# The gated experts' second matmul with the activations stationary, summed out of PSUM by VectorE

## The chip, the cores and the metric

One core of a Trainium2 chip runs the whole program. Times are device microseconds of that core. PE is TensorE, DVE is VectorE, ACT is ScalarE, POOL is GpSimd, and SP is the engine whose queue issues the DMAs.

## The reference

There are 1152 tokens of 512 features. They come from an attention with a window of 64 keys (2 sequences of 576, 8 heads of 64). Two feed-forward layers follow:

```
x = attention(q, k, v)                       # 1152 x 512
p = domain_probs / sum(domain_probs)         # 1152 x 4
for e in range(4):                           # gated experts, F = 1024
    out += p[:, e:e+1] * (relu(x @ w1[e]) @ w2[e])
h = out @ w_in                               # 512 -> 2048
return (h * cos(h)) @ w_out                  # 2048 -> 512
```

All is float32, except that `w_in` and `w_out` arrive as float64.

## The kernel before

**Precision.** Each operand of a large matmul is split into two parts, a rounded high part (`hi`) and the rest (`lo`), and a product is three matmuls: high by high, high by low, low by high. ACT makes the high part of each weight (L164, `whi`), and POOL, for all units but one, the low part (L170, `wlo`).

**Passes.** The work is cut into passes (e, g). Index e counts slices of 512 hidden features: 0 to 7 for the gated experts (two for each), 8 to 11 for the last layer. Index g is a group of tokens: group 0 has 256, group 1 has 384, group 2 has 512. Passes 0 and 1 go over the groups one by one, while the attention still makes the later groups' tokens. From pass 2 on each e goes over all three groups, in turn backward and forward, so that two passes over group 0, or two over group 2, follow each other at every turn. Passes 7 and 8 both go forward.

**Steps.** A pass has four steps (f), each of 128 hidden features. `emit_a` is the first matmul of a step: 12 matmuls with the weight stationary and the group's tokens moving (L457 to L459), into one of four PSUM banks of the pool `psa`. The gated experts then take the relu on ACT (`hh`, L466) and its low part on DVE (`hl`, L467). The last layer takes h cos(h) in several pieces (`cos_stages`), and holds its `psa` bank until the product `gg` is made (L491). `emit_b` is the second matmul of a step (L525). It adds into PSUM banks of the pool `psb`, which has four; after the last step `finish` evicts them.

**Orientation of the second matmul.** For e below 8 the weight is stationary and the token group moves: four blocks of 128 output features, each over n tokens, so four banks for any group, and a result with features on the partitions. DVE multiplies each block with a broadcast row of the gate values (L555, at pass 0 L552), and POOL adds it to the sum (L556). The broadcast rows, `pb`, are made from a transposed copy of the gates in DRAM, and loaded by `load_pb` on SP's queue, one for each pass. After pass 7 `split_x` splits the sum, block by block, into the next layer's `xhi` and `xlo` (L534, L535). For e from 8 the activations are stationary and the weight moves: one block of 128 tokens by 512 features for each 128 tokens, so 2, 3 and 4 banks.

**Order.** Every engine works in the order in which the program is written. The order between passes is a fixed sequence of ticks, one for each `emit_a` or `emit_b`:

```
            ("A", i, 2), ("A", i, 3), ("B", i, 0), ("B", i, 1),
            ("A", i + 1, 0), ("B", i, 2), ("A", i + 1, 1), ("B", i, 3),
```

Between the last second matmul of a pass and the first of the next stand two first matmuls. `later(d, fn)` puts a piece of work d ticks behind the present one. `between(part)` is called inside a tick, after a part of its matmuls, and lets in pieces that are due and, in the first 30 ticks, pieces of the attention. From tick 32 on one of the 16 float64 weight units is converted every 9 ticks, by seven DVE instructions (L130 to L153).

Of the kernel before, what the change touches and what calls it, by code (L numbers as in the profile page):

```python
# [8 lines left out]
F32 = mybir.dt.float32  # L9
# [4 lines left out]
ALU = mybir.AluOpType  # L14
# [10 lines left out]
def tile_window_attention_moe_cosglu(  # L25
# [12 lines left out]
    nc = tc.nc  # L38
    P = 128
# [5 lines left out]
    NT = NTOK // P  # L45
    NE, DM, FF = w1.shape
    NP = H // 2
    KD = DM // P
    FE = 512
    NFC = FE // P  # L50
    SPL = FF // FE
    NM = NE * SPL
    NX = NM + w_in.shape[1] // FE
    SCALE = 1.0 / float(D) ** 0.5
    GS = [256, 384, 512]
    G0 = [0, 256, 640]
# [5 lines left out]
    rawp = ctx.enter_context(tc.tile_pool(name="rawp", bufs=4))  # L62
    xp = ctx.enter_context(tc.tile_pool(name="xp", bufs=1))
    hp = ctx.enter_context(tc.tile_pool(name="hp", bufs=5))
    pbp = ctx.enter_context(tc.tile_pool(name="pbp", bufs=2))
    tp = ctx.enter_context(tc.tile_pool(name="tp", bufs=4))
    dramp = ctx.enter_context(tc.tile_pool(name="dramp", bufs=1, space=bass.MemoryType.DRAM))
    psb = ctx.enter_context(tc.tile_pool(name="psb", bufs=4, space=bass.MemoryType.PSUM))
    psa = ctx.enter_context(tc.tile_pool(name="psa", bufs=4, space=bass.MemoryType.PSUM))
# [3 lines left out]
    def bank(name):  # L73
        return psa.tile([P, 512], F32, tag="psa", name=name)
# [168 lines left out]
        nc.sync.dma_start(out=t[:n], in_=v[b, s + W - n:s + W, :])  # L243
        v_t[j] = t

    ident = acon.tile([P, P], F32, name="ident")
    mask = acon.tile([P, 1, 2 * W], F32, name="mask")
    mask0 = acon.tile([P, 1, W], F32, name="mask0")

# [21 lines left out]
    xhi, xlo = {}, {}  # L271
# [98 lines left out]
            nc.vector.tensor_tensor(out=lo, in0=src, in1=hi.bitcast(F32), op=ALU.subtract)  # L370


    pT = dramp.tile([NT * NE, P], F32, name="pT")
    pb_t = {}

    dpn = acon.tile([P, NT, NE], F32, name="dpn")

    def load_gate():
# [2 lines left out]
    def gate():  # L381
        t = dpn
        s = acon.tile([P, NT], F32, name="dps")
        nc.vector.tensor_reduce(out=s, in_=t, op=ALU.add, axis=AX.X)
        nc.vector.tensor_scalar_add(s, s, 1e-09)
        r = acon.tile([P, NT, 1], F32, name="dpr")
        nc.vector.reciprocal(out=r[:, :, 0], in_=s)
        pn = acon.tile([P, NT, NE], F32, name="dpp")
        nc.vector.tensor_tensor(out=pn, in0=t, in1=r.to_broadcast([P, NT, NE]), op=ALU.mult)
        return pn  # L390

    def store_gate(pn):
        ps = bank("psg")
        nc.tensor.transpose(
            out=ps[:NT * NE, :P], in_=pn.rearrange("p c e -> p (c e)"), identity=ident
        )
        pt = acon.tile([P, P], F32, name="dpt")
        nc.vector.tensor_copy(out=pt[:NT * NE], in_=ps[:NT * NE, :P])
        nc.sync.dma_start(out=pT, in_=pt[:NT * NE])

    def load_pb(e, g):
        t = pbp.tile([P, GS[g]], F32, tag="pb", name="pb")
        c0, n = G0[g] // P, GS[g] // P
        src = pT.rearrange("(c e) t -> e c t", e=NE)[e // SPL, c0:c0 + n, :]
        nc.sync.dma_start(
            out=t.rearrange("p (c t) -> p c t", c=n), in_=src.partition_broadcast(P)
        )
        pb_t[e, g] = t


    bias_m = const.tile([P, 1], F32, name="bias_m")
# [26 lines left out]
    def later(d, fn, *args):  # L438
        waiting.append((tick[0] + 1 + d, fn, args))
# [65 lines left out]
    def emit_b(s):  # L505
        e, g, f = steps[s]
        n = GS[g]
        u, fo = divmod(f, 2)
        whi, wlo = w_hi[e, 1, u], w_lo[e, 1, u]
        hh, hl = h_t.pop(s)  # L510
        first, last = f == 0, f == NFC - 1
        no = KD if e < NM else n // P
        if first:
            b_ps[g] = [psb.tile([P, 512], F32, tag="psb", name="pb_acc") for _ in range(no)]
        for i in range(no):
            if e < NM:
                ps = b_ps[g][i][:, :n]
                cs = slice(P * i, P * (i + 1))
                ops = ((whi[:, fo, cs], hh), (whi[:, fo, cs], hl), (wlo[:, fo, cs], hh))
            else:  # L520
                ps = b_ps[g][i]
                cs = slice(P * i, P * (i + 1))
                ops = ((hh[:, cs], whi[:, fo, :]), (hh[:, cs], wlo[:, fo, :]), (hl[:, cs], whi[:, fo, :]))
            for m, (a, b) in enumerate(ops):
                nc.tensor.matmul(  # L525
                    out=ps, lhsT=a, rhs=b, start=first and m == 0, stop=last and m == 2
                )
            between((i + 1) / no)
        if last:
            finish(e, g)  # L530

    def split_x(g, i):
        a = acc_x[g][:, i, :]
        nc.scalar.copy(out=xhi[g][:, i, :], in_=a)  # L534
        nc.vector.tensor_tensor(  # L535
            out=xlo[g][:, i, :], in0=a, in1=xhi[g][:, i, :].bitcast(F32), op=ALU.subtract
        )

    def finish(e, g):
        n = GS[g]  # L540
        pss = b_ps.pop(g)
        if e < NM:
            pb = pb_t.pop((e, g))
            if e == 0:
                acc[g] = xp.tile([P, KD, n], F32, tag=f"acc{g}", name="acc")
            if e == NM - 1:
                x_tiles(g)
                acc_x[g] = acc[g]
            for i in range(KD):
                a = acc[g][:, i, :]  # L550
                if e == 0:
                    nc.vector.tensor_tensor(out=a, in0=pss[i][:, :n], in1=pb, op=ALU.mult)  # L552
                    continue
                t = tp.tile([P, 512], F32, tag="t", name="t")[:, :n]
                nc.vector.tensor_tensor(out=t, in0=pss[i][:, :n], in1=pb, op=ALU.mult)  # L555
                nc.gpsimd.tensor_tensor(out=a, in0=a, in1=t, op=ALU.add)  # L556
                if e == NM - 1:
                    later(2 + i, split_x, g, i)
        else:
            if e == NM:  # L560
                acc[g] = xp.tile([P, KD, n], F32, tag=f"acc{g}", name="acc")
            av = acc[g].rearrange("p k n -> p (k n)").rearrange("p (i m) -> p i m", m=DM)
            for i in range(n // P):
                if e == NX - 1:
                    r0 = G0[g] + i * P
                    for cs in (slice(0, DM // 2), slice(DM // 2, DM)):
                        nc.vector.tensor_tensor(
                            out=av[:, i, cs], in0=av[:, i, cs], in1=pss[i][:, cs], op=ALU.add
                        )
                        nc.sync.dma_start(out=out[r0:r0 + P, cs], in_=av[:, i, cs])  # L570
                elif e == NM:
                    nc.scalar.copy(out=av[:, i, :], in_=pss[i])
                else:
                    nc.vector.tensor_tensor(out=av[:, i, :], in0=av[:, i, :], in1=pss[i], op=ALU.add)
# [103 lines left out]
    for t, (what, s) in enumerate(seq):  # L678
# [4 lines left out]
            pool_of["cos"] = actx.enter_context(tc.tile_pool(name="cosp", bufs=3))  # L683
        if what == "A":
            emit_a(s)
            e, g, f = steps[s]
            if f == 3 and e < NM and s > NFC:
                nx = order[s // NFC + 1]
                if nx[0] < NM:
                    load_pb(*nx)  # L690
        else:
            emit_b(s)
        issue_upto(t + 1)
# [3 lines left out]
            actx.close()  # L697
            pool_of["w64"] = actx.enter_context(tc.tile_pool(name="w64", bufs=2))
        if t == 2:
            pn = gate()  # L700
        if t == 5:
            store_gate(pn)
            load_pb(*order[0])
            load_pb(*order[1])
        conversions(t)
        weights(t)
    issue_upto(len(seq) + NB)
# [39 lines left out]
```

## Time and profile before

| | us |
|---|---|
| median of 3 runs | 677.43 (677.15 to 679.08) |
| profiled execution | 677.95 |
| its span | 676.2 |
| PE busy | 651.4 |
| DVE busy | 444.9 |
| POOL busy | 265.8 |
| ACT busy | 248.0 |

The span is the time from the first to the last instruction in the profile; the execution's own time is 1.75 us longer. A busy PE is not PE at its peak, because matmuls overlap: how far apart they start is read from the chain or from the timeline, where a row "2.88 PE pb_acc L525 x24" says that 24 matmuls followed each other in 2.88 us.

### The profile page before, as it was taken

To read this page: it belongs to the slowest core of one execution; us is meant where nothing else is said; L and a number is where in the kernel's file an instruction comes from. 1 tells how busy PE (TensorE), PEld (TensorE's weight loads), DVE (VectorE), ACT (ScalarE), POOL (GpSimd) and SP (SyncE) were. 2 spreads that over 40 slices of the span, in tenths; PEclk is the share of its full clock that TensorE was granted. 3 is DMA by queue.
4 is the path that set the end of the run, shared out by engine and by line. 5 is a ranking of instruction groups with operands and counts; after the bars stand their busy time and mean duration, and the time that the engine had idled before them with its cause. 6 is when DMAs were issued, how large, how long until landed. Compare 5 with 4: busy or idle time off the path is not lost.

```text
span 676.2 us, 9533 instructions
## 1 busy us (share of the span) xinstructions
PE 651.4 (96%) x3673; PEld 588.5 (87%) x3673; DVE 444.9 (66%) x682; ACT 248.0 (37%) x539; POOL 265.8 (39%) x199
## 2 busy tenths in 40 slices
PE   5889999999999899999999999999999999899997
PEld 4888999888899898899998899988888898788896
DVE  4668763245779963778966659754856657854655
ACT  4556451212123112113112113225665755654443
POOL 6776530512666634736632636733402202200000
PEclk9979999999999999999999999999999999999999
DMA  9747213304145544223642433421201100000012
GB/s 271 236 119 216 70 29 110 128 28 156 50 156 164 168 141 171 84 78 116 221 162 98 167 96 129 156 101 63 63 1 62 45 18 1 1 0 1 1 62 79
DMA packets 46012, 67.89 MB, mean 100 GB/s; under 512 B 3820, under 2 KB 29456, under 8 KB 45968
## 3 DMA queue, kind: packets, MB, share of 16 engines
q1 hardware_dynamic: 45968, 67.29, 30.7%
q8 instruction: 29, 0.48, 0.3%
q14 instruction: 15, 0.12, 0.1%
HBM read 56.51 MB, written 10.77 MB: 99 GB/s over the span
## 4 chain that ended last, share of the span: by engine, by line
PE 84%; DVE 7%; DMA 3%; ACT 2%; POOL 2%; issue 1%; SPq 0%; DVEq 0%; POOLq 0%; ACTq 0%
PE pb_acc L525 41%; PE ph L459 13%; PE ph L458 13%; PE ph L457 13%; PE psv L347 2%; PE pss L285 2%; DMA vr<-in_v_dram 1%; DMA raw<-in_moe_w_in_dram 1%; DVE kk L481 1%; POOL qbd L218 1%; DMA kT<-in_k_dram 1%; ACT e L307 1%; DVE hl L497 1%; DVE hl L467 1%; POOL e L321 1%
## 5 line engine op out<-in xcount | busy, mean ns | idle before, releaser
L457 PE MATMUL ph<-xhi,whi 128*128 128x256 f32 (+2 forms) x576 | 195.3, 339 | 0.0
L459 PE MATMUL ph<-xhi,wlo 128*128 128x256 f32 (+2 forms) x576 | 193.8, 336 | 0.0
L458 PE MATMUL ph<-xlo,whi 128*128 128x256 f32 (+2 forms) x576 | 193.8, 336 | 0.0
L170 POOL TENSOR_TENSOR wlo<-raw,whi 128x1024 fp32r<-128x1024 f32 x47 | 125.9, 2688 | 108.8 <-ACT whi L164 108.5
L556 POOL TENSOR_TENSOR acc<-acc,t 128x256 f32<-128x256 f32 (+2 forms) x84 | 97.2, 1190 | 175.6 <-DVE t L555 175.6
L466 ACT ACTIVATE hh<-ph 128x256 fp32r<-128x256 f32 (+2 forms) x96 | 47.0, 491 | 288.0 <-PE ph L459 288.0
L525 PE MATMUL pb_acc<-hh,whi 128*128 128x256 f32 (+2 forms) x384 | 130.5, 340 | 4.2 <-DVE t L555 4.2
L525 PE MATMUL pb_acc<-hh,wlo 128*128 128x256 f32 (+2 forms) x384 | 129.2, 337 | 0.0
L525 PE MATMUL pb_acc<-hl,whi 128*128 128x256 f32 (+2 forms) x384 | 129.2, 336 | 0.0
L467 DVE SCALAR_TENSOR_TENSOR hl<-ph,hh 128x256 fp32r<-128x256 f32 (+2 forms) x96 | 52.4, 553 | 115.7 <-ACT hh L466 115.6
L458 PEld LDWEIGHTS ph<-xlo,whi 128*128 128x128 f32 x576 | 109.1, 189 | 8.6
L457 PEld LDWEIGHTS ph<-xhi,whi 128*128 128x128 f32 x576 | 109.1, 189 | 8.6
L459 PEld LDWEIGHTS ph<-xhi,wlo 128*128 128x128 f32 x576 | 109.0, 189 | 7.5
L525 PEld LDWEIGHTS pb_acc<-hh,whi 128*128 128x128 f32 x384 | 72.8, 190 | 10.2 <-issue 3.1
L525 PEld LDWEIGHTS pb_acc<-hl,whi 128*128 128x128 f32 x384 | 72.8, 190 | 5.1
L525 PEld LDWEIGHTS pb_acc<-hh,wlo 128*128 128x128 f32 x384 | 72.7, 189 | 5.0
L525 PE MATMUL pb_acc<-whi,hl 128*128 128x512 f32 x144 | 56.7, 394 | 2.0 <-DVE hl L497 2.0
L525 PE MATMUL pb_acc<-whi,hh 128*128 128x512 f32 x144 | 56.5, 392 | 0.9 <-ACT hh L494 0.9
L525 PE MATMUL pb_acc<-wlo,hh 128*128 128x512 f32 x144 | 56.4, 392 | 0.0
L164 ACT ACTIVATE whi<-raw 128x1024 fp32r<-128x1024 f32 x48 | 50.4, 1052 | 9.8 <-DMA raw<-in_moe_w_dram 9.8
L481 DVE TENSOR_SCALAR kk<-kk 128x256 f32<-128x256 f32 (+2 forms) x48 | 25.3, 527 | 37.4 <-ACT kk L480 37.3
L497 DVE TENSOR_TENSOR hl<-gg,hh 128x256 fp32r<-128x256 f32 (+2 forms) x48 | 36.0, 749 | 18.5 <-ACT hh L494 18.5
(64 smaller groups left out, 752.3 us busy)
## 6 DMA issues: line engine op xcount, KB each, us to landing
raw<-in_moe_w_dram SPq DMA_DIRECT2D x32, 512.0 KB, 6.2
raw<-in_moe_w_in_dram SPq DMA_DIRECT2D x8, 1024.0 KB, 7.1
w<-r SPq DMA_DIRECT2D x16, 512.0 KB, 3.0
raw<-in_moe_w_out_dram SPq DMA_DIRECT2D x8, 1024.0 KB, 8.0
raw<-w SPq DMA_DIRECT2D x16, 512.0 KB, 3.3
vr<-in_v_dram SPq DMA_DIRECT2D x16, 256.0 KB, 4.1
qraw<-in_q_dram SPq DMA_DIRECT2D x18, 128.0 KB, 3.9
out_dram<-acc SPq DMA_DIRECT2D x18, 128.0 KB, 1.8
```

What stands on the lines that cost most here:

```text
L164: nc.scalar.activation(out=hi, in_=raw_t[n], func=AF.Copy)
L170: engine.tensor_tensor(out=lo, in0=t, in1=w_hi[units[n]].bitcast(F32), op=ALU.subtract)
L285: nc.tensor.matmul(out=pv[:, p], lhsT=qbd[j % NQB][:, p, :], rhs=kt[:, p, :], start=True, stop=True)
L457: nc.tensor.matmul(out=ps, lhsT=whi[:, d, cs], rhs=xh[:, d, :], start=d == 0, stop=False)
L458: nc.tensor.matmul(out=ps, lhsT=whi[:, d, cs], rhs=xl[:, d, :], start=False, stop=False)
L459: nc.tensor.matmul(out=ps, lhsT=wlo[:, d, cs], rhs=xh[:, d, :], start=False, stop=d == KD - 1)
L466: nc.scalar.activation(out=hh, in_=ps, func=AF.Relu)
L467: nc.vector.scalar_tensor_tensor(out=hl, in0=ps, scalar=0.0, in1=hh.bitcast(F32), op0=ALU.max, op1=ALU.subtract)
L481: nc.vector.tensor_scalar_add(kk, kk, -MAGIC)
L497: nc.vector.tensor_tensor(out=hl, in0=gg, in1=hh.bitcast(F32), op=ALU.subtract)
L525: nc.tensor.matmul(out=ps, lhsT=a, rhs=b, start=first and m == 0, stop=last and m == 2)
L556: nc.gpsimd.tensor_tensor(out=a, in0=a, in1=t, op=ALU.add)
```

## The change

For the gated experts the second matmul takes the form of the last layer's: `hh` and `hl` are stationary, w2 moves, and a block is 128 tokens by 512 features. The gate is then one value per partition, so the normalized gates stay in SBUF (`gate_p`) and the broadcast rows, their DRAM copy, their loads and the transposition that made them go. DVE multiplies a block out of PSUM with its gate and adds it to the sum in one instruction, and POOL's additions go. The sum has tokens on the partitions, so after pass 7 PE transposes each block of 128 tokens (`turn_x`, four transposes into one `psa` bank), and `split_x` splits it out of PSUM half a tick later. The pools `pbp` and `tp` go, and the identity for the transposes moves into a pool that stays open.

```diff
-    ident = acon.tile([P, P], F32, name="ident")
+    ident = const.tile([P, P], F32, name="ident")
...
-        no = KD if e < NM else n // P
+        no = n // P
...
-            if e < NM:
-                ps = b_ps[g][i][:, :n]
-                cs = slice(P * i, P * (i + 1))
-                ops = ((whi[:, fo, cs], hh), (whi[:, fo, cs], hl), (wlo[:, fo, cs], hh))
-            else:
-                ps = b_ps[g][i]
-                cs = slice(P * i, P * (i + 1))
-                ops = ((hh[:, cs], whi[:, fo, :]), (hh[:, cs], wlo[:, fo, :]), (hl[:, cs], whi[:, fo, :]))
+            ps = b_ps[g][i]
+            cs = slice(P * i, P * (i + 1))
+            ops = ((hh[:, cs], whi[:, fo, :]), (hh[:, cs], wlo[:, fo, :]), (hl[:, cs], whi[:, fo, :]))
...
-    def split_x(g, i):
-        a = acc_x[g][:, i, :]
-        nc.scalar.copy(out=xhi[g][:, i, :], in_=a)
+    def turn_x(g, i):
+        ps = bank("psx")
+        pv = ps.rearrange("d (k t) -> d k t", k=KD)
+        for k in range(KD):
+            nc.tensor.transpose(
+                out=pv[:, k, :], in_=acc_x[g][:, i, P * k:P * (k + 1)], identity=ident
+            )
+        later(0.5, split_x, g, i, pv)
+
+    def split_x(g, i, pv):
+        cs = slice(P * i, P * (i + 1))
+        nc.scalar.copy(out=xhi[g][:, :, cs], in_=pv)
         nc.vector.tensor_tensor(
-            out=xlo[g][:, i, :], in0=a, in1=xhi[g][:, i, :].bitcast(F32), op=ALU.subtract
+            out=xlo[g][:, :, cs], in0=pv, in1=xhi[g][:, :, cs].bitcast(F32), op=ALU.subtract
         )
...
-            pb = pb_t.pop((e, g))
             if e == 0:
-                acc[g] = xp.tile([P, KD, n], F32, tag=f"acc{g}", name="acc")
+                acc[g] = xp.tile([P, n // P, DM], F32, tag=f"acc{g}", name="acc")
...
-            for i in range(KD):
+            for i in range(n // P):
                 a = acc[g][:, i, :]
+                c = G0[g] // P + i
+                p = gate_p[:, c, e // SPL:e // SPL + 1]
                 if e == 0:
-                    nc.vector.tensor_tensor(out=a, in0=pss[i][:, :n], in1=pb, op=ALU.mult)
+                    nc.vector.tensor_scalar(out=a, in0=pss[i], scalar1=p, scalar2=None, op0=ALU.mult)
                     continue
-                t = tp.tile([P, 512], F32, tag="t", name="t")[:, :n]
-                nc.vector.tensor_tensor(out=t, in0=pss[i][:, :n], in1=pb, op=ALU.mult)
-                nc.gpsimd.tensor_tensor(out=a, in0=a, in1=t, op=ALU.add)
+                nc.vector.scalar_tensor_tensor(
+                    out=a, in0=pss[i], scalar=p, in1=a, op0=ALU.mult, op1=ALU.add
+                )
                 if e == NM - 1:
-                    later(2 + i, split_x, g, i)
+                    later(1 + i, turn_x, g, i)
...
         if t == 2:
-            pn = gate()
-        if t == 5:
-            store_gate(pn)
-            load_pb(*order[0])
-            load_pb(*order[1])
+            gate()
```

## Rows read from the trace of the kernel before

**Rows 1.** The page's summary: busy us (share of the span) xinstructions.

```profile
PE 651.4 (96%) x3673; PEld 588.5 (87%) x3673; DVE 444.9 (66%) x682; ACT 248.0 (37%) x539; POOL 265.8 (39%) x199
```

**Rows 2.** Stretches: length; PE, PEld, DVE, ACT, POOL busy; PEclk, DMA share, GB/s.

```profile
111.50:205.60 94.10, 94.10 (x464) 82.67 (x463) 50.28 (x58) 18.94 (x28) 35.54 (x20) 1.00 0.32 109
205.60:221.80 16.20, 13.79 (x116) 13.61 (x115) 15.56 (x17) 5.14 (x9) 10.65 (x7) 1.00 0.54 171
```

**Rows 3.** Waits of PE, whole span: us in total, times, longest.

```profile
PE pb_acc L525 <- DVE t L555: 4.2, 4, 2.4
```

**Rows 4.** Timeline of PE: start, us, instruction, [idle before it, releaser]; five restarts.

```profile
221.78 0.36 PE L525 MATMUL pb_acc<-hh,whi 128*128 128x256 f32 x1 [2.41 <-DVE t L555]
221.97 0.28 PE L525 MATMUL pb_acc<-hl,whi 128*128 128x256 f32 x1
...
322.73 0.36 PE L525 MATMUL pb_acc<-hh,whi 128*128 128x256 f32 x1 [0.58 <-DVE t L555]
...
337.29 0.41 PE L525 MATMUL pb_acc<-hh,whi 128*128 128x384 f32 x1 [0.26 <-DVE t L555]
...
424.52 0.36 PE L525 MATMUL pb_acc<-hh,whi 128*128 128x256 f32 x1 [0.93 <-DVE t L555]
...
480.64 0.50 PE L525 MATMUL pb_acc<-whi,hh 128*128 128x512 f32 x1 [0.92 <-ACT hh L494]
```

**Rows 5.** The chain that ended last: start, us, engine, tile, line, matmuls.

```profile
88.22 0.44 PE pst L331 x4
...
130.92 5.44 PE pb_acc L525 x24
...
193.79 4.16 PE pb_acc L525 x24
...
310.63 2.88 PE pb_acc L525 x24
...
661.70 2.07 PE pb_acc L525 x9
```

**Rows 6.** Timeline of DVE at the seam of passes 2 and 3 over group 0.

```profile
214.45 3.31 DVE L142 SCALAR_TENSOR_TENSOR r<-raw,x 128x1024 f32<-128x1024 uint32 x1
217.69 0.41 DVE L467 SCALAR_TENSOR_TENSOR hl<-ph,hh 128x256 fp32r<-128x256 f32 x1
...
219.75 0.41 DVE L467 SCALAR_TENSOR_TENSOR hl<-ph,hh 128x256 fp32r<-128x256 f32 x1
...
221.22 1.40 DVE L555 TENSOR_TENSOR t<-pb_acc,pb 128x256 f32<-128x256 f32 x4
222.55 0.74 DVE L467 SCALAR_TENSOR_TENSOR hl<-ph,hh 128x256 fp32r<-128x256 f32 x2
```

**Rows 7.** Groups by line and shape: xcount | busy us, mean ns | idle before, releaser.

```profile
L556 POOL TENSOR_TENSOR acc<-acc,t 128x256 f32<-128x256 f32 (+2 forms) x84 | 97.2, 1190 | 175.6 <-DVE t L555 175.6
...
L555 DVE TENSOR_TENSOR t<-pb_acc,pb 128x512 f32<-128x512 f32 x28 | 17.4, 682 | 0.0
...
L482 DVE SCALAR_TENSOR_TENSOR r<-kk,ph 128x512 f32<-128x512 f32 x16 | 11.0, 687 | 0.6
```

**Rows 8.** Timeline of POOL, ACT and DVE where the last layer begins.

```profile
471.56 5.29 POOL L556 TENSOR_TENSOR acc<-acc,t 128x512 f32<-128x512 f32 x4 [8.07 <-DVE t L555]
...
473.47 0.47 ACT L480 ACTIVATE kk<-ph,bias_m 128x256 f32<-128x256 f32 x1 [0.97 <-PE ph L459]
...
474.31 0.42 DVE L482 SCALAR_TENSOR_TENSOR r<-kk,ph 128x256 f32<-128x256 f32 x1
...
477.38 2.44 DVE L535 TENSOR_TENSOR xlo<-acc,xhi 128x512 fp32r<-128x512 f32 x1
479.74 0.41 DVE L491 TENSOR_TENSOR gg<-ph,r 128x256 f32<-128x256 f32 x1
480.08 0.68 DVE L535 TENSOR_TENSOR xlo<-acc,xhi 128x512 fp32r<-128x512 f32 x1
```

**Rows 9.** Stretches of the attention, columns as in rows 2.

```profile
36.20:43.00 6.80, 6.16 (x29) 6.12 (x30) 2.61 (x7) 1.72 (x6) 5.19 (x5) 0.50 0.30 82
...
60.00:112.00 52.00, 51.80 (x375) 51.05 (x374) 35.12 (x78) 24.61 (x93) 20.22 (x27) 1.00 0.23 67
```

More of the change, by code (lines that the diff above doesn't have):

```diff
@@ L64, in tile_window_attention_moe_cosglu @@
     hp = ctx.enter_context(tc.tile_pool(name="hp", bufs=5))
-    pbp = ctx.enter_context(tc.tile_pool(name="pbp", bufs=2))
-    tp = ctx.enter_context(tc.tile_pool(name="tp", bufs=4))
     dramp = ctx.enter_context(tc.tile_pool(name="dramp", bufs=1, space=bass.MemoryType.DRAM))
@@ L370, in att_x @@
             nc.vector.tensor_tensor(out=lo, in0=src, in1=hi.bitcast(F32), op=ALU.subtract)
-    pT = dramp.tile([NT * NE, P], F32, name="pT")
-    pb_t = {}
+    gate_p = const.tile([P, NT, NE], F32, name="gate_p")
     dpn = acon.tile([P, NT, NE], F32, name="dpn")
@@ L387, in gate @@
         nc.vector.reciprocal(out=r[:, :, 0], in_=s)
[L388 to L408, printed above, removed]
+        nc.vector.tensor_tensor(out=gate_p, in0=t, in1=r.to_broadcast([P, NT, NE]), op=ALU.mult)
     bias_m = const.tile([P, 1], F32, name="bias_m")
@@ L548, in finish @@
                 acc_x[g] = acc[g]
-            for i in range(KD):
+            for i in range(n // P):
                 a = acc[g][:, i, :]
+                c = G0[g] // P + i
+                p = gate_p[:, c, e // SPL:e // SPL + 1]
                 if e == 0:
-                    nc.vector.tensor_tensor(out=a, in0=pss[i][:, :n], in1=pb, op=ALU.mult)
+                    nc.vector.tensor_scalar(out=a, in0=pss[i], scalar1=p, scalar2=None, op0=ALU.mult)
                     continue
-                t = tp.tile([P, 512], F32, tag="t", name="t")[:, :n]
-                nc.vector.tensor_tensor(out=t, in0=pss[i][:, :n], in1=pb, op=ALU.mult)
-                nc.gpsimd.tensor_tensor(out=a, in0=a, in1=t, op=ALU.add)
+                nc.vector.scalar_tensor_tensor(
+                    out=a, in0=pss[i], scalar=p, in1=a, op0=ALU.mult, op1=ALU.add
+                )
                 if e == NM - 1:
-                    later(2 + i, split_x, g, i)
+                    later(1 + i, turn_x, g, i)
         else:
             if e == NM:
-                acc[g] = xp.tile([P, KD, n], F32, tag=f"acc{g}", name="acc")
-            av = acc[g].rearrange("p k n -> p (k n)").rearrange("p (i m) -> p i m", m=DM)
+                acc[g] = xp.tile([P, n // P, DM], F32, tag=f"acc{g}", name="acc")
+            av = acc[g]
             for i in range(n // P):
@@ L685, in tile_window_attention_moe_cosglu @@
             emit_a(s)
[L686 to L690, printed above, removed]
         else:
```

## The prediction

> **What bounds the kernel now.** I read the page's summary first, then the stretches, then what PE waited for, then the chain. PE is busy for 651.4 of 676.2 us [rows 1], no other engine passes 445, and the chain that ended last runs over PE. Read by stretch the same holds: from 111.5 to 205.6 us PE is busy without a gap, while around 213 us, where two passes over the smallest token group follow each other, PE loses 2.4 us and DVE is busy for 15.56 of 16.2 us [rows 2]. So the kernel pays for every PE instruction behind the first 110 us, and beside that for a few waits. The list of waits has the largest of them outside the attention: 4.2 us, in four places, of the second matmul for the eviction of its PSUM banks [rows 3]. Three of the four (2.41, 0.58 and 0.93 us) stand at such a seam of two passes over the small group, the fourth (0.26 us at 337) where group 1 follows group 0; a wait of another kind, 0.92 us for hh, stands where the last layer begins [rows 4]. The change touches the PE stream, these four waits, and that beginning.
>
> **Part 1, the second matmul of the eight gated passes.** One step (one f) of group 0 has 12 matmuls of 256 columns, of group 1 12 of 384, of group 2 12 of 512. After it they are 6, 9 and 12 of 512: the same columns, fewer instructions. From start to start one takes 2.88/24 = 120.0 ns at 256 columns, 4.16/24 = 173.3 at 384, 5.44/24 = 226.7 at 512 [rows 5]: 13.3 ns for each instruction beside its columns at the full clock. A step of group 0 becomes 1.44 - 1.36 = 0.08 us shorter, one of group 1 2.08 - 2.04 = 0.04; there are 8 x 4 steps of each, so 32 x 0.12 = 3.84 us. The last layer already runs this form, and there nine matmuls also come at 2.07 us, 230 ns each [rows 5]; by that the gain is 32 x (0.06 + 0.01) = 2.24 us. I take 3.4, nearer the first, since the stretches without other stalls show it.
>
> **Part 2, the turn.** The sum over the experts now lies with tokens on the partitions, and the last layer's first matmul needs features there. So behind pass 7 PE transposes nine blocks of 128 tokens, four transposes each. The attention has the same instruction, fp32, 128 columns, in groups of four; one group takes 0.44 us of the chain [rows 5]. 9 x 0.44 = 4.0 us, on the path, since PE has no gaps there; nothing hides them. (Their lower bound is 0: had PE been waiting anyway. The upper is part 4's.) The one transpose of the gates goes, with its copy and its store: 0.1 us.
>
> **Part 3, the eviction.** Before, DVE made four products per step and POOL added them: 84 adds, 97.2 us of POOL [rows 7]. After, DVE makes one instruction for each token block, reading PSUM, a scalar and the sum. A two-input DVE instruction of 512 columns from PSUM takes 687 ns, the product of 512 took 682 [rows 7], so group 2 stays, and group 0 goes from 1.40 us for four [rows 6] to 2 x 0.69 = 1.37. DVE is neither relieved nor loaded, and POOL's relief is worth nothing by itself: the waits of PE behind the attention that I found name DVE and ACT alone [rows 4].
>
> What counts is how many of the four PSUM banks a pass takes. Before, every pass took all four, so the next could not begin until the first eviction ran. After, group 0 takes two and group 1 three. At the seam of two passes over group 0 the second finds two banks that were evicted a whole pass earlier; in the wait at 337 us, from group 0 to group 1, the first two banks are free as well. So the wait for the eviction goes. Next in line is hl of the new pass: at 221 us hl of its first two steps ran at 217.69 and 219.75, ahead of the eviction at 221.22, and hl of the next two at 222.55 [rows 6]. PE, starting at 219.4, would need the second of them at 220.7 and the third behind another first matmul, after 224: all are there. So the whole 4.2 us go, and 4.4 with the slow first matmul behind each wait (0.36 us in the rows of the restarts, [rows 4], against the usual 0.28). The bounds are 0 (hl late in turn) and 4.8. Taken: 4.4.
>
> **Part 4, what the turn makes wait.** Each turn takes a bank of the four that the first matmul also uses, waits for the new sum on DVE, and is split by one ACT copy and one DVE subtraction, both out of PSUM. PE is in order, so a turn that waits holds every matmul behind it. For groups 0 and 1 one whole first matmul lies between the eviction and the turn (2.1 and 2.7 us): I count 0.3 us, for group 0, where the conversions share DVE. For group 2 the turns fall into the beginning of the last layer. There a bank is held from the first matmul to the product with the cosine: ACT began at 473.47, the product ended at 480.15, 6.7 us later [rows 8]. The third turn needs this bank and comes, by PE's own work (a turn 0.44, a first matmul 1.44, a turn 0.44, a second matmul 1.36, together 3.7 us), near 477.2. Of the 6.7 us, 2.44 are one subtraction that is 0.68 when undisturbed [rows 8]; with that short the product ends near 478.4, so the turn waits some 1.2 us, and the 0.92 us for hh that were there go. Net +0.3, bounded by -0.9 (bank free in time) and +2.0 (product as late as before). Together +0.6.
>
> That the subtraction becomes short is a point on ports. In the rows, an instruction with both inputs in SBUF took 2.44 us while POOL was at work, and one with an input in PSUM, at 474.31, took 0.42 during a POOL add [rows 8]. The Trainium skill, page "SBUF — State Buffer", section "Who interferes with whom", says that only a DVE instruction with two SBUF inputs, or in a two-port mode, contends with GpSimd; the new subtraction and the new sum each have one. By the rule part 4 is +0.6 us; were PSUM readers caught too, it would be 1.8 us more for each one caught. The trace agrees with the rule as far as one row can.
>
> **Part 5, the rest.** The loads of the broadcast gates leave SP's queue; the waits of PE above name no DMA, so that is worth nothing. The finer points of the attention's order move: its pieces are let in between blocks of the second matmul, now at halves and thirds of a step, not quarters. In the first 15 steps that is six second matmuls; a piece moved by a quarter of 1.4 us, six times, bounds it by 2 us to either side. I take 0.
>
> **Sum.** -3.4 + 4.0 - 0.1 - 4.4 + 0.6 = -3.3 us. The profiled execution took 677.95 us (span 676.2 and 1.75 around it), which gives 674.65; it is 0.5 above the runs' median, 677.43, and from that it is 674.1. That is what I predict.
>
> **Rivals.**
> A. The bank waits only change their name: DVE, 96% busy at 205 to 222 us, is the true limit there, and PE waits for hl in place of the bank. For it: the busy share. Against: hl stands ahead of the eviction in DVE's order, by the rows above. Then -3.4 + 4.0 - 0.1 + 0.6 = +1.1: 678.5.
> B. Slower. The turns of pass 7 wait for DVE: the sum stands behind a piece of the weight conversion on DVE, in order, and each turn stops PE. One such piece took 3.3 us beside POOL [rows 6]; against the 2.1 us of cover it holds a turn by 1.2, and a late product by up to 2.9 (477.2 to 480.15). Without any turn wait the sum is -3.9, so the side changes when the nine turns lose 3.9 us together and the loss can be told from noise at 5.9. With four turns losing 1.75 (2.44 - 0.69) it is +3.1: 680.5. Against: most of the conversion is through by then, and the PSUM readers aren't caught.
> C. The half-clock stretch of the attention goes. From 36.2 to 43.0 us the granted clock was 0.50 (1.2 GHz); PE was busy for 6.16 us of it [rows 9], so half of that, 3.1 us, is what the lower level cost. Before it PE runs the second matmul of group 0, whose shape changes. If it goes: 671.0. If a second such stretch comes (D), 677.2. The turn itself could be its place: from 60 to 112 us such groups ran between matmuls, the one at 88.22 [rows 5] among them, at a clock of 1.00 [rows 9], so I give that little. The Trainium skill, page "TensorE: Matmul & The Clock Gate", section "Part 4: PE-mode transpose", says that transposes don't count as a busy engine for the gate in the same way; one lower stretch at the turn would be D's 677.2, and the rows from 60 to 112 speak against it for groups as short as these.
>
> **How the numbers follow.** Forecast 0.50, with 672.6 to 675.8 of its own (part 1 at either end, -0.4 and +1.2 us, and part 4 at -0.9 or a wait or two more); A 0.18; B 0.12; C 0.12; D 0.08. A measurement of this kernel tells about 0.3%, 2.0 us, from no change: faster is below 675.4, slower above 679.5. Faster: 0.44 of the forecast and C, 0.56. Same: 0.06 of the forecast, A and D, 0.32. Slower: B, 0.12. The range, 670.5 to 679.5, leaves out B and a C with more than its own gain.
>
> **What would show it.** Right: second matmuls of group 0 at 1.36 to 1.39 us for six; no wait for an eviction behind 200 us; nine groups of transposes of 0.44 us between 430 and 490 us; one wait of a turn, for the product, at the start of the last layer. Wrong: hl or hh named in place of the evictions at the three seams (A); waits of the turns for the sum or the bank that add up to over 6 us (B); another clock in the first 60 us (C, D). If the stretch from 112 to 430 us is not shorter by about 7 us, my parts 1 and 3 are wrong.

## The result, and the profile after

| | before | after |
|---|---|---|
| median of the runs (us) | 678.22 (6 runs) | 671.32 (6 runs) |
| profiled execution (us) | 677.95 | 670.79 |
| its span (us) | 676.2 | 669.0 |

The ratio is 0.9901, with a 95% interval of 0.9883 to 0.9919: the changed kernel is 6.7 us faster (5.5 to 7.9). Run again later, it gave 0.9902 (0.9884 to 0.9920). The forecast was faster by 3.3 us, 674.1, with a range of 670.5 to 679.5: the gain is twice what I worked out.

The page's summary of the changed kernel, to be read against [rows 1]: PE has lost 3.5 us, POOL 106.

```profile
PE 647.9 (97%) x3420; PEld 565.9 (85%) x3420; DVE 425.1 (64%) x654; ACT 248.2 (37%) x536; POOL 159.9 (24%) x115
```

All that PE waited for in the changed kernel (in total, times, longest); the row of [rows 3] has no successor, and neither has the wait for hh of [rows 4]:

```profile
PE pss L283 <- POOL qbd L216: 10.9, 7, 5.5
PE pst L329 <- POOL e L319: 3.8, 4, 1.6
PE pb_acc L497 <- DVE hl L474: 2.0, 1, 2.0
PE psx L509 <- DVE acc L537: 0.2, 1, 0.2
```

**Where the time went.** I cut both traces at the first matmul of the same passes, so that a row of one answers to a row of the other (columns as in rows 2). Before, from the first matmul of pass (0, 0) to the last layer's end:

```profile
24.63:69.64 45.01, 41.44 (x321) 39.75 (x319) 33.23 (x71) 25.02 (x90) 29.82 (x30) 0.92 0.58 176
...
210.57:224.73 14.16, 11.75 (x99) 11.57 (x98) 14.06 (x16) 3.42 (x6) 9.13 (x6) 1.00 0.50 164
...
313.35:341.53 28.18, 27.34 (x195) 26.88 (x194) 28.01 (x30) 5.39 (x10) 18.96 (x12) 1.00 0.45 149
...
414.79:427.47 12.68, 11.75 (x99) 11.57 (x98) 11.78 (x15) 3.43 (x6) 8.99 (x5) 1.00 0.63 228
427.47:477.45 49.98, 49.98 (x278) 45.58 (x277) 29.30 (x51) 17.52 (x34) 25.78 (x19) 1.00 0.24 81
477.45:494.22 16.77, 15.85 (x79) 13.81 (x78) 13.45 (x22) 12.02 (x24) 4.20 (x2) 1.00 0.20 64
```

The same stretches of the changed kernel:

```profile
25.09:67.07 41.98, 37.89 (x283) 34.42 (x282) 33.40 (x68) 24.88 (x89) 29.67 (x30) 1.00 0.58 178
...
207.75:219.01 11.26, 11.26 (x73) 10.26 (x72) 11.19 (x11) 3.44 (x6) 5.22 (x3) 1.00 0.26 100
...
307.09:333.60 26.51, 26.51 (x151) 24.24 (x150) 23.45 (x28) 5.52 (x10) 6.88 (x3) 1.00 0.52 179
...
406.42:417.68 11.26, 11.26 (x73) 10.26 (x72) 8.60 (x10) 3.44 (x6) 5.29 (x3) 1.00 0.66 234
417.68:471.74 54.06, 53.84 (x290) 46.89 (x288) 31.75 (x50) 19.20 (x36) 8.46 (x4) 1.00 0.23 79
471.74:487.06 15.32, 15.32 (x81) 14.05 (x80) 10.53 (x19) 10.64 (x20) 2.40 (x1) 1.00 0.12 35
```

Down the six rows: the attention is 3.03 us shorter, and its granted clock is 1.00 where it was 0.92; the next three, with the seams, are 2.90, 1.67 and 1.42 shorter, and PE is busy without a gap in them; the fifth, with most of the turns, is 4.08 longer; the last, the beginning of the last layer, is 1.45 shorter. What is not shown, the start of the kernel and four stretches, is 0.81 shorter together. The sum is -7.2 us, the difference of the two spans. From pass (0, 2) to pass (7, 1), 115.54 to 427.47 us before and 113.17 to 417.68 after, the kernel is 7.4 us shorter, where the prediction asked for about 7 between 112 and 430.

### The profile page after: what moved, and what is told of

Its sections match the earlier page's. It is cut to its first block, busy times and chain, and to the rows that moved or that the text cites. A ratio compares the mean times of both kernels' runs of the same rounds, so it can differ in the third digit from the quotient of the medians.

```text
span 669.0 us, 8785 instructions
## 1 busy us (share of the span) xinstructions
PE 647.9 (97%) x3420; PEld 565.9 (85%) x3420; DVE 425.1 (64%) x654; ACT 248.2 (37%) x536; POOL 159.9 (24%) x115
## 4 chain that ended last, share of the span: by engine, by line
PE 89%; DVE 4%; ACT 2%; POOL 2%; DMA 1%; issue 1%; SPq 0%; DVEq 0%; POOLq 0%; ACTq 0%
PE pb_acc L497 42%; PE ph L436 14%; PE ph L435 14%; PE ph L434 14%; PE pss L283 2%; PE psv L345 2%; POOL qbd L216 1%; DMA qraw<-in_q_dram 1%; ACT e L305 1%; DVE kk L458 1%; PE psx L509 1%; PE pst L329 1%; POOL e L319 1%; DVE hl L474 0%; ACT whi L162 0%
## 5 line engine op out<-in xcount | busy, mean ns | idle before, releaser
L497 PE MATMUL pb_acc<-whi,hl 128*128 128x512 f32 x432 | 169.1, 391 | 2.0 <-DVE hl L474 2.0
L497 PE MATMUL pb_acc<-whi,hh 128*128 128x512 f32 x432 | 170.2, 394 | 0.0
L497 PE MATMUL pb_acc<-wlo,hh 128*128 128x512 f32 x432 | 169.0, 391 | 0.0
L497 PEld LDWEIGHTS pb_acc<-whi,hl 128*128 128x128 f32 x432 | 81.1, 188 | 20.3 <-DVE hl L474 3.2
L497 PEld LDWEIGHTS pb_acc<-whi,hh 128*128 128x128 f32 x432 | 81.3, 188 | 15.0 <-ACT hh L471 0.7
L497 PEld LDWEIGHTS pb_acc<-wlo,hh 128*128 128x128 f32 x432 | 81.3, 188 | 14.1
L457 ACT ACTIVATE kk<-ph,bias_m 128x256 f32<-128x256 f32 (+2 forms) x48 | 27.8, 580 | 51.8 <-PE ph L436 51.8
L537 DVE SCALAR_TENSOR_TENSOR acc<-pb_acc,gate_p,acc 128x512 f32<-128x512 f32 x63 | 43.3, 742 | 0.0
L468 DVE TENSOR_TENSOR gg<-ph,r 128x256 f32<-128x256 f32 (+2 forms) x48 | 26.6, 554 | 22.0 <-ACT r L465 21.1
L464 ACT ACTIVATE r<-r 128x256 f32<-128x256 f32 (+2 forms) x48 | 25.2, 525 | 26.1 <-DVE r L459 25.9
```

The lines of the kernel that those rows point to most:

```text
L457: nc.scalar.activation(out=kk, in_=ps, func=AF.Identity, bias=bias_m, scale=1.0 / TWO_PI)
L497: nc.tensor.matmul(out=ps, lhsT=a, rhs=b, start=first and m == 0, stop=last and m == 2)
L537: nc.vector.scalar_tensor_tensor(out=a, in0=pss[i], scalar=p, in1=a, op0=ALU.mult, op1=ALU.add)
```

## The experiments

**The kernel before once more.** Is the half-clock stretch of the attention part of its order, or chance?

> The kernel before, unchanged, so that each of its executions comes with its granted clock. Theory (the half-clock stretch near 36 to 43 us belongs to the old order of the attention): its runs show a mean clock of about 0.994 and 677 to 679 us, and nearly none of them 1.000. Rival (the stretch comes and goes by chance, and the one profile had it): clocks between 0.99 and 1.00, and the runs at 1.00 are some 3 us shorter than the others, near 674.

677.97 us, ratio 0.9996 (0.9983 to 1.0009). The profiled one (span 676.8) had a half-clock stretch from 16.8 to 23.6 us, in place of 36.2 to 43.0, and a second one right behind the seam's wait. Stretches of this execution, (0, 0) to (0, 1) and the second stretch:

```profile
25.86:68.74 42.88, 38.86 (x319) 37.02 (x318) 34.12 (x73) 25.01 (x90) 29.21 (x30) 1.00 0.61 190
221.60:225.00 3.40, 3.40 (x18) 3.40 (x18) 3.37 (x5) 0.00 (x0) 3.40 (x4) 0.50 1.01 280
209.67:225.31 15.64, 13.23 (x98) 13.05 (x97) 15.39 (x16) 3.42 (x6) 10.61 (x7) 0.89 0.55 174
```

So two things are separated. At full clock the attention's stretch is 42.88 us before and 41.98 after: at most 0.9 of the 3.03 us belong to the change, and 2.1 to the clock of that one execution. (The 42.88 hold a PE wait of 0.5 us for xlo at 26.75 that the other trace hasn't; another pair, further down, gives 0.24.) And the seam can cost more than its wait: 15.64 us with 3.4 us at half clock behind it, 14.16 without. The theory is half right: the stretch comes in different places. The rival's run without one did not come: none of this kernel's 12 times lies under 676.85, and none of their mean clocks above 0.997.

**Four banks reserved.** A pass's block list was made four long, whatever it used.

```diff
-            b_ps[g] = [psb.tile([P, 512], F32, tag="psb", name="pb_acc") for _ in range(no)]
+            b_ps[g] = [psb.tile([P, 512], F32, tag="psb", name="pb_acc") for _ in range(KD if e < NM else no)]
```

> The changed kernel, but each gated pass reserves four PSUM banks, as before, and uses two, three or four of them. Theory (the waits at the seams went because group 0 takes two banks and group 1 three): the waits of the second matmul for the eviction come back at the seams of group 0, near 210, 305 and 400 us, 4 to 5 us in all, and the time is 675 to 676. Rival (they went because POOL's additions no longer disturb DVE, or because DVE has less to evict): no such wait, and 671 as changed.

670.81 us, ratio 0.9891 (0.9872 to 0.9910). The experiment was badly made: nothing writes the added tiles, and PE's instructions, and its waits behind the attention, came out the same as in the changed kernel. It says nothing of banks; it is one more measurement of the changed kernel.

**Group 0 in halves.** In passes 2 to 7 group 0 again has 12 matmuls of 256 columns a step, in four half-used banks.

```diff
-        no = n // P
+        w = DM // 2 if g == 0 and 2 <= e < NM else DM
+        no = n // P * DM // w
...
-            ps = b_ps[g][i]
-            cs = slice(P * i, P * (i + 1))
-            ops = ((hh[:, cs], whi[:, fo, :]), (hh[:, cs], wlo[:, fo, :]), (hl[:, cs], whi[:, fo, :]))
+            ps = b_ps[g][i][:, :w]
+            j, m0 = divmod(i * w, DM)
+            cs, ms = slice(P * j, P * (j + 1)), slice(m0, m0 + w)
+            ops = ((hh[:, cs], whi[:, fo, ms]), (hh[:, cs], wlo[:, fo, ms]), (hl[:, cs], whi[:, fo, ms]))
```

> The changed kernel, but in passes 2 to 7 the second matmul of group 0 moves w2 in halves of 256 columns into four half-used banks, so 12 matmuls a step as before instead of 6, and four evictions of 256. Theory: the seam waits come back as with four banks (4 to 5 us), and each step of group 0 costs 0.06 to 0.08 us more, 24 steps, 1.5 to 1.9 us: 676.5 to 678. The instruction's own cost is read as the difference to the kernel with four banks, 1.5 to 1.9 us (13.3 ns for each of 144 matmuls would be 1.9). Rival (fewer matmuls buy nothing, since PE's columns are the same): equal to the kernel with four banks.

676.69 us, ratio 0.9978 (0.9967 to 0.9990). A step of group 0, 12 matmuls, in the chain of this kernel, and then one of the changed kernel, 6 matmuls:

```profile
213.47 1.44 PE pb_acc L499 x12
```

```profile
212.17 1.39 PE pb_acc L497 x6
```

Fewer instructions buy time at equal columns: 0.05 us a step, which over 24 steps is 1.2 us, less than the 1.5 to 1.9 expected. Two of the four waits of before came back, 1.4 us at the first seam and 1.2 at the third; the seam of passes 4 and 5 and the wait behind it stayed away, with four banks in use. (The first is put down to ACT's whi, but PE went on at 219.15 and that whi ended at 219.16; DVE's four evictions there ran from 218.53.) So the banks are not the whole story. The next three kernels cross the two candidates.

**Banks and POOL, crossed.** In the first, block i always takes bank i, so that nothing rotates; in the second DVE writes the product to SBUF and POOL adds, as before, with banks rotating; the third has both.

```diff
-            b_ps[g] = [psb.tile([P, 512], F32, tag="psb", name="pb_acc") for _ in range(no)]
+            b_ps[g] = [psb.tile([P, 512], F32, tag=f"psb{i}", name="pb_acc") for i in range(no)]
```

```diff
-                nc.vector.scalar_tensor_tensor(
-                    out=a, in0=pss[i], scalar=p, in1=a, op0=ALU.mult, op1=ALU.add
-                )
+                t = tp.tile([P, 512], F32, tag="t", name="t")
+                nc.vector.tensor_scalar(out=t, in0=pss[i], scalar1=p, scalar2=None, op0=ALU.mult)
+                nc.gpsimd.tensor_tensor(out=a, in0=a, in1=t, op=ALU.add)
```

> The changed kernel, but block i of every second matmul always goes to PSUM bank i, so a pass finds its banks as the pass just before left them. (Reserving four banks without using them, the kernel e1_four_banks, gave the very same instructions and waits as the changed kernel, so it tested nothing.) Theory (the seam waits went because group 0 rotates over free banks): waits of the second matmul for the eviction at the seams near 210, 310 and 408 us come back, 2.5 to 4.5 us in all, 674 to 676. Rival (they went because POOL's additions, which disturbed DVE, are gone): no such waits, 671. A share for each is possible: with four half-banks the first and the third of the three seams waited, 1.5 and 1.3 us, and the second did not.

> The changed kernel, but DVE writes the gated product out of PSUM to SBUF and POOL adds it to the sum, as before; the banks rotate as in the changed kernel. Theory (banks): no wait for an eviction at the seams, 671 to 672; at the beginning of the last layer, and for the turns, which now wait for POOL's sum, up to 2 us more: 671 to 673.5. Rival (POOL's relief made the gain at the seams): hl late there, PE waits of 3 to 5 us near 210, 310 and 408 us, 674 to 676.

> The changed kernel with both: block i always in bank i, and POOL adds. Theory (banks alone): as with the same banks alone at the seams. Rival (banks and POOL's additions each hold a share): the seam waits of the kernel before come back in full, 4 to 5 us, which is more than with either of the two alone.

| | banks rotate | block i in bank i |
|---|---|---|
| POOL doesn't add | 671.32, ratio 0.9901 | 676.04, ratio 0.9976 (0.9963 to 0.9989) |
| POOL adds | 679.80, ratio 1.0027 (1.0011 to 1.0044) | 682.77, ratio 1.0070 (1.0057 to 1.0082) |

Waits of PE for an eviction or for the sum: same banks, then POOL adds, then both. (In the first the row for whi stands for the eviction too: the wait ended at 420.24, and DVE's two evictions there ran from 419.35; whi ended at 420.12, so the two can't be told apart by this row alone.)

```profile
PE pb_acc L497 <- DVE acc L537: 1.9, 1, 1.9
PE pb_acc L497 <- ACT whi L162: 1.5, 1, 1.5
```

```profile
PE psx L510 <- POOL acc L540: 3.3, 1, 3.3
...
PE pb_acc L498 <- DVE t L539: 1.8, 2, 1.0
```

```profile
PE pb_acc L498 <- DVE t L539: 6.8, 4, 3.2
...
PE psx L510 <- POOL acc L540: 1.6, 1, 1.6
```

Where these waits stand decides what they say. At the three seams of two passes over group 0 PE waits 3.4 us with the same banks (1.9 at the first, 1.5 at the third), not at all when POOL adds and the banks rotate, and 6.1 with both (3.18, 1.31 and 1.58; the other 0.8 of the 6.8 stand at 336.46, where group 1 follows). In the last two kernels DVE's eviction at the first seam is equally late: it begins 23.59 us behind the first matmul of pass (2, 0), which starts at 194.93 with rotating banks and at 194.63 without. With rotating banks PE goes on; without, it waits. DVE with rotating banks, then DVE and PE with both:

```profile
218.52 1.40 DVE L539 TENSOR_SCALAR t<-pb_acc,gate_p 128x512 f32<-128x512 f32 x2
```

```profile
218.22 1.39 DVE L539 TENSOR_SCALAR t<-pb_acc,gate_p 128x512 f32<-128x512 f32 x2
...
219.10 0.75 PE L498 MATMUL pb_acc<-whi,hh 128*128 128x512 f32 x1 [3.18 <-DVE t L539]
```

So at the seams the theory of banks holds: rotating alone takes the wait away. POOL's relief alone only makes it shorter, 3.4 for 6.1 us. Beyond the seams the theory is refuted. The 1.8 us stand where group 1 follows group 0, at 232.50 and 332.97, before the third of group 1's three blocks; two banks were free, and the third is one that group 0's pass has just left:

```profile
231.71 0.74 DVE L539 TENSOR_SCALAR t<-pb_acc,gate_p 128x512 f32<-128x512 f32 x1
...
232.50 0.50 PE L498 MATMUL pb_acc<-whi,hh 128*128 128x512 f32 x1 [1.01 <-DVE t L539]
```

In the changed kernel DVE makes this eviction 8.5 us behind the first matmul of pass (3, 1), at 227.53; here it is 12.9 us. The largest single effect is one I had priced at nothing: with POOL adding, a turn waits 3.3 us for POOL's sum. PE stood from 429.2 us on; DVE's product began at 430.26, behind two pieces of the conversion, and POOL's add could begin only then:

```profile
430.26 1.40 DVE L539 TENSOR_SCALAR t<-pb_acc,gate_p 128x512 f32<-128x512 f32 x2
431.15 2.95 POOL L540 TENSOR_TENSOR acc<-acc,t 128x512 f32<-128x512 f32 x2 [2.61 <-DVE t L539]
```

Behind that wait PE ran at half clock, in the same execution:

```profile
431.70:438.50 6.80, 6.03 (x22) 5.84 (x22) 5.03 (x6) 1.27 (x3) 2.40 (x2) 0.50 0.01 2
```

The time with POOL adding, 679.80, lies outside both forecasts, and is 0.3% more than before. Part of it is the clock: its 12 executions run from 676.73 at a mean clock of 0.999 to 682.15 at 0.989.

**The turn left out.** The sum is split as it lies, so the last layer's input is not the reference's.

```diff
-                    later(1 + i, turn_x, g, i)
+                    later(1.5 + i, split_x, g, i, acc_x[g][:, i, :].rearrange("p (k t) -> p k t", k=KD))
```

> The changed kernel without the transposes behind pass 7: the sum is split as it lies, out of SBUF, so the last layer's input is not the reference's. Theory (the turn costs its PE time and next to no wait, 9 x 0.35 to 0.44 us, 3.2 to 4.0, plus 0.4 for one wait): 667 to 668. Rival 1 (the turn costs more through the banks and waits it makes): under 666. Rival 2 (without the turn the old wait for hh at the beginning of the last layer, 1.1 us, and slow steps there return, because the subtraction again reads SBUF twice beside POOL): 668.5 to 669.5, with a wait named hh or hl near 470 us.

668.64 us (666.0 to 670.57 in 5 runs), ratio 0.9846 (0.9822 to 0.9870). The times scatter too much for a few us, and the profiled execution had a half-clock stretch in the attention, so I read the stretch from pass (7, 0) to pass (8, 2), at full clock in both: 487.06 - 406.42 = 80.64 us with the turn, and without it

```profile
409.16:485.31 76.15, 76.15 (x404) 67.61 (x402) 49.91 (x75) 32.89 (x61) 16.14 (x7) 1.00 0.28 97
```

The turn costs 4.49 us, against 4.0 + 0.3 in the prediction for the transposes and group 0's wait. The median lies where rival 2 had it, but rival 2 is refuted: the wait for hh doesn't return, though the subtraction reads SBUF twice again. None of its nine meets POOL there, and none takes over 694 ns. With POOL adding and the subtraction out of PSUM it didn't return either (no wait for hh in that kernel's list): three of the nine ran beside POOL's adds, and took 678 to 683 ns. Either part of the change is enough to take it away.

**What the trace points to.** First the gates: in the changed kernel as before, one tiny DVE instruction of their normalization takes 1.70 us beside a POOL weight split, and holds up the softmax of a block. Put ahead of the first step, on both kernels:

```diff
+    gate()
     for t, (what, s) in enumerate(seq):
...
-        if t == 2:
-            gate()
```

> The changed kernel with the normalization of the gates ahead of the first expert step, and nothing else. In the kernel with both moves PE's wait at 33.5 us fell from 1.25 to 0.35 us and the wait of 1.7 us behind it stayed. Theory: 0.9 us off, 670.0 to 670.6. Rival (the next wait takes it up, or a half-clock stretch comes): 671 or more.

669.70 us, ratio 0.9881 (0.9863 to 0.9899); the changed kernel, run beside it, had 671.94 and 0.9902. The instruction now takes 0.3 us. Its group in the changed kernel, then in this one:

```profile
L382 DVE TENSOR_SCALAR dps<-dps 128x9 f32<-128x9 f32 x1 | 1.7, 1697 | 0.0
```

```profile
L382 DVE TENSOR_SCALAR dps<-dps 128x9 f32<-128x9 f32 x1 | 0.3, 295 | 0.0
```

The transposes that wait behind it, by the timelines, in the same order:

```profile
35.14 0.66 PE L329 MATMUL pst<-ident,e 128*128 128x128 f32 x4 [1.07 <-POOL e L319]
```

```profile
33.46 0.66 PE L329 MATMUL pst<-ident,e 128*128 128x128 f32 x4 [0.18 <-POOL e L319]
```

PE's wait is 0.9 us shorter, as expected. From pass (0, 0) to (0, 1) it takes 41.15 us for the changed kernel's 41.98, and from there to the end 601.9 in both profiles; so the move is worth 0.8 us, and the rest of the 2.2 between the medians is in neither stretch. The same move on the kernel before:

> The kernel before with the normalization of the gates ahead of the first expert step, and nothing else. Theory (half-clock stretches follow waits of PE, so a shorter wait at 33 us has fewer of them behind it): 675 to 677, 1 to 3 us less than before, of which 0.9 is the wait itself. Rival (the stretch near 36 us comes whatever stands before it): 677.0 to 677.6, the wait alone. If it reached 673 or less, most of the change's gain would have been the clock of the attention.

676.94 us, ratio 0.9982 (0.9970 to 0.9995), 1.2 us less, at the border of theory and rival. Its attention had no half-clock stretch in the profiled execution. From (0, 0) to (0, 1), this kernel and then the changed one with the same move:

```profile
25.02:66.41 41.39, 38.56 (x321) 36.92 (x319) 32.87 (x71) 25.04 (x90) 29.80 (x30) 1.00 0.62 190
```

```profile
24.31:65.46 41.15, 37.98 (x284) 34.47 (x282) 33.06 (x68) 24.86 (x89) 29.70 (x30) 1.00 0.59 180
```

But the stretch behind the seam was there again:

```profile
207.34:222.98 15.64, 13.23 (x98) 13.06 (x97) 15.37 (x16) 3.43 (x6) 10.61 (x7) 0.89 0.55 172
```

With its attention clean, the kernel before is still 7.1 us of span behind the changed kernel with the same move (674.5 and 667.4), 1.5 of them by the half-clock stretch at the seam: the change's gain is not the clock of the attention, and 0.24 us of it lie there.

Then a subtraction in the cosine that takes 2.20 us beside a weight split on POOL, at 569.82 us in the changed kernel, and 0.28 elsewhere, moved to ACT; first everywhere and with the gates ahead, then in passes 8 to 10 only.

```diff
-        nc.vector.tensor_scalar_add(kk, kk, -MAGIC)
+        nc.scalar.activation(out=kk, in_=kk, func=AF.Identity, bias=bias_n, scale=1.0)
```

> The changed kernel with two moves that its trace suggests: the normalization of the gates (four small DVE instructions, one of which waits 1.70 us beside POOL at 31 us and holds up the softmax of an attention block behind it) goes ahead of the first expert step; and in the last layer the subtraction of the rounding constant goes from DVE, where it waits for POOL's weight split (2.2 us at the seam near 569 us), to ACT. Expected if both are on the path: the waits of PE at 34 to 37 us shrink from 3.0 to about 1.7 us, the wait of 2.2 us near 570 us goes: 667.5 to 668.5. If PE then waits for the next in line (POOL's copies for the queries; ACT, which gains 48 instructions of 0.4 to 0.6 us): 670 to 671.

669.76 us, ratio 0.9881 (0.9868 to 0.9894), between the two forecasts. The wait at 570 us shrank from 2.0 to 0.8 us, and a new one of 0.4 us for ACT's hh came in pass 11. The profiled execution had a half-clock stretch of 3.4 us in the attention.

> The gates ahead, and the subtraction of the rounding constant on ACT in passes 8 to 10 only; in pass 11, where no weight is split any more and POOL is idle, it stays on DVE. Against the kernel with both moves, where a new wait of 0.5 us stood at 661 us: 0.4 us less, 669.0 to 669.5. Rival (that wait has another cause): 669.8.

669.06 us, ratio 0.9865 (0.9843 to 0.9886); the wait in pass 11 is gone, as expected. This is the fastest kernel here. It beats the kernel before clearly, and the changed kernel run beside it by 2.9 us in the medians, with intervals that touch (0.9884 is the lower end there). From pass (0, 1) to the end, at full clock in both but for the last 3 us, its profile has 600.6 us for 601.9.

**The changed kernel once more**, beside the last three.

> The changed kernel unchanged, beside the three others of this job. 670 to 672. Theory (its gain has two parts: some 5.5 us of PE time and waits, which every execution has, and 1 to 2 us because half-clock stretches follow long waits of PE and it has fewer of those): its profile shows at most one half-clock stretch before the end, in the attention or behind the wait near 570 us, and with one it is some 1.7 us longer than the 669.0 us of span without. Rival (the half-clock stretches of the kernel before were chance): two or three stretches here too, and 673 or more.

671.94 us, ratio 0.9902 (0.9884 to 0.9920). Its profile, like the first and like the four-banks one, has no half-clock stretch between 24 us and the last 3 us; the span is 668.8. But its five times spread from 670.61 to 672.64, and one of the first six was 675.0 with a mean clock of 0.991, so it meets such stretches in some executions. The theory holds for the profiles; how often each kernel meets one is read from the mean clocks, in the next section.

## Why the prediction was right or wrong

**Part 1 (3.4 us less) held.** Over passes 2 to 7 a step of group 0 fell from 1.445 to 1.381 us in the mean, one of group 1 from 2.091 to 2.059 (starts of PE's instructions in the two timelines): 24 x (0.064 + 0.032) = 2.3 us, of which 0.3 are the slow first matmuls behind the four waits. If the 8 steps of either group in passes 0 and 1 gained the same, which the attention's waits hide, it is 32 x 0.096 = 3.1.

**Part 2 (4.0 us more) held.** Nine groups of four transposes stand between 427 and 472 us, at 0.35 to 0.41 us, with the slow first matmul behind each; leaving them out with their one wait saves 4.49.

**Part 3 (4.4 us less) held in size, and in reason at the seams only.** The four waits went, 4.8 us from start to start. hl was there in time, as I had read from [rows 6], and rival A fell. That rotating banks take the seams' waits away is shown by the crossed experiment, with DVE equally late. Two steps failed. I wrote that POOL's relief is worth nothing by itself: with POOL adding the kernel loses 1.8 us before evictions and 3.3 before a turn. And for the wait at 337 us I counted two free banks and left out the third that group 1 needs; its eviction is in time only with POOL relieved. The reason can be seen on DVE, which makes the evictions: its conversion pieces are shorter when POOL adds nothing. DVE from 200 to 440 us, first before:

```profile
L147 DVE TENSOR_TENSOR r<-r,m 128x1024 f32<-128x1024 f32 x13 | 22.1, 1703 | 0.0
...
L139 DVE TENSOR_SCALAR x<-m 128x1024 uint32<-128x1024 uint32 x14 | 13.8, 989 | 0.2
```

then after:

```profile
L145 DVE TENSOR_TENSOR r<-r,m 128x1024 f32<-128x1024 f32 x13 | 18.2, 1399 | 0.0
...
L137 DVE TENSOR_SCALAR x<-m 128x1024 uint32<-128x1024 uint32 x13 | 8.9, 687 | 0.2
```

and in the changed kernel with POOL adding:

```profile
L146 DVE TENSOR_TENSOR r<-r,m 128x1024 f32<-128x1024 f32 x14 | 20.3, 1449 | 0.0
...
L138 DVE TENSOR_SCALAR x<-m 128x1024 uint32<-128x1024 uint32 x13 | 16.7, 1283 | 0.2
```

The seven means of a weight unit add up to 9.9 us before, 8.6 after, 8.6 with the same banks alone, and 10.5 with POOL adding. I had looked for POOL in the waits of PE, where it doesn't stand; it stands a step behind, in the durations of the DVE instructions ahead of the one that PE waits for. The Trainium skill, page "SBUF — State Buffer", section "Who interferes with whom", says that a DVE instruction with two SBUF inputs contends with a GpSimd instruction that reads SBUF. The traces agree: the two costliest such pieces of the conversion (L132 and L140 in the changed kernel) take 1713 ns each in the mean, and 2005 and 2015 with POOL adding. I used the rule for the new instructions and not for the old ones that stay. DVE's new eviction was also dearer than I had it, 742 ns and not 687.

**Part 4 (0.6 us more) failed in its second half.** Group 0's turn waited, 0.22 us by its row and 0.38 from start to start, against 0.3. The wait of 1.2 us at the third turn of group 2 did not come. The timeline of the changed kernel has the third turn at 469.55 and the product whose bank it should have waited for at 470.37:

```profile
468.42 0.68 DVE L517 TENSOR_TENSOR xlo<-psx,xhi 128x512 fp32r<-128x512 f32 x1
...
469.55 0.60 PE L509 MATMUL psx<-ident,acc 128*128 128x128 f32 x4
...
470.37 0.41 DVE L468 TENSOR_TENSOR gg<-ph,r 128x256 f32<-128x256 f32 x1
```

So it did not take that bank. I had assumed that banks go round in the order of requests; by these rows it can have had the first turn's, read out at 469.1 by the subtraction above. And the old stall there went whole, 1.45 us of the stretch with its slow steps, not 0.92. The term is -1.1 instead of +0.6. The short subtraction was right, 684 ns in the mean and at most 692, but none of the nine ran beside POOL here; that POOL doesn't stretch it is shown by the three that did with POOL adding. The new eviction reads PSUM too: 46 of its 72 ran at least in part beside POOL, and none took over 751 ns.

**What the sum lacked is the clock.** The terms as measured are -3.1 + 4.1 - 0.1 - 4.8 - 1.1 = -5.0 us, against -3.3 forecast (4.1 is the turn's 4.49 without group 0's wait; the 0.1 for the gates' transposition is the forecast's, not measured). Readings at equal clock agree. From pass (0, 1) to the end the first two profiles, at full clock there but for the last 3 us, have 606.5 and 601.9 us, 4.6 less, and the attention adds 0.2 to 0.9. Executions with a mean clock of 0.997 have a median span of 675.2 us before (9 of them) and 670.2 after (5, the four-banks kernel counted in), 5.0 less. The rest of the measured 6.7 is what half-clock stretches cost the kernel before more often than this one: of its 74 executions with a clock on record none lies above 0.997, of 16 of the changed kernel, counted in the same way, eight lie at 0.999 or 1.000. I had this as rival C, at 0.12, and for the attention alone. The runs show a second place, behind the seam's wait of 2.4 us: 1.5 us in two of the three profiled executions that have this wait. So beside "C 0.12" the forecast should have held a price for the stretches that follow PE's waits. Rival B did not come in this kernel. With POOL adding it did, 679.8, near the 680.5 I gave it, though by one turn and not four: PE's wait is put down to POOL's sum, and that stood behind DVE's product and the conversion, as B has it.

Why the stretches come is open. Kernels with a PE wait of over 1 us between 200 and 440 us have 4 of 125 executions at 0.999 or above (the kernel before, with the gates ahead too, group 0 in halves, and the three crossed ones); the others have 17 of 34. But in the profiles of two of the former (group 0 in halves, same banks alone) the stretch stands in the attention, near 38 us, and not behind the wait. Of the profiled executions with the wait of 2.0 us near 570 us in the last layer, three show a half-clock stretch behind it (with POOL adding, with both, without the turn) and nine don't. So that a wait taken away takes its stretch with it is argued, not shown.

## What to carry to other kernels

An engine that no wait names can still set the end: look at the durations of the instructions ahead of those that are waited for, and at what ran beside the long ones. When two causes are crossed, read where each wait stands before adding them up: here the totals suggested two shares at the seams, and the places showed that rotating banks alone take those waits away. A change that puts a consumer closer behind a producer (here the turn behind the sum) may need another of its parts to pay at all: with POOL's additions kept, this one is a loss of 0.3%. And price a long wait of PE with the clock that may follow it, not with its length alone.

## What the runs showed of the hardware that I had not expected

A PE wait of 2.4 us was followed by 3.4 us at half clock (1.2 GHz) in two of three executions, one of 3.2 us by 3.4 (same banks and POOL adding), one of 3.3 us by 6.8; the waits of 1.2 to 1.9 us between 200 and 440 us by none. The 3.4 us at the lower level behind the seam cost 1.5 us. A DVE instruction of nine elements per partition took 1.70 us beside a POOL instruction and 0.30 without. A DVE instruction with one operand in PSUM, one in SBUF and a scalar per partition, 512 columns, took 742 ns, where one with a constant in the scalar's place took 687 [rows 7].
